# A new order of the transfers and of the first work in a fused S4 and gMLP block

## Chip, cores and metric

The kernel runs on one core of one Trainium2 chip. The metric is the time of one execution on the device, in microseconds (us); of several runs the median counts.

## What is computed

The reference, cut to the parts that matter here (`_A_ref` is a diagonal state-space layer as a convolution of length 2048, `_B_ref` a gated MLP with a 2048x2048 spatial mix):

```python
def _A_ref(u, A_re, A_im, B_re, B_im, C_re, C_im, log_dt, Dskip):
    dt = jnp.exp(log_dt)[:, None]
    P = jnp.exp((dt * A)[:, :, None] * l[None, None, :])
    K = jnp.einsum("dn,dnl,dn->dl", Cc, P, dB).real
    y = irfft(rfft(u) * rfft(K))[:L]
    return y + u * Dskip
mod = (_silu(c) @ w_mod).reshape(c.shape[0], 6, 1, -1)
sa, ca, ga, sb, cb, gb = mod
h = _layernorm(x) * (1 + ca) + sa
x = x + ga * _A_ref(h, ...)
h = _layernorm(x) * (1 + cb) + sb
x = x + gb * _B_ref(h, ...)
```

There are 2048 rows of 576 channels with 128 complex poles each; `w_mod` is 576 x 3456.

## The kernel before

The convolution is done as a transform in two stages of 32 and 64 points. The poles' parameters come in five groups of channels (four of 128, one of 64); `poles` turns them on VectorE and ScalarE into phases and logarithms of magnitudes, splits each into three bf16 parts and writes these to DRAM (`pa_d`, `pb_d`), from where `poles_load` fetches the tables `lb`, `lc`, `la` of one group. Group 0 is worked off by itself first, groups 1 to 3 together (432 columns wide) by the steps `q`.

Everything up to the tick loop (line 862) is the opening. Its work is listed by hand in the string `OPENING`, one short step after another, and each engine runs its instructions in exactly that order (line 154 pins it). The steps that matter:

- `mm k`, `me k`, `mo k`, `mf k`: modulation vector k: matmuls with `w_mod`, copy, matmul with ones, final form (`gar`, `cga`, `sga`). `ga`, `gb` split the shift into `gsp` (ScalarE) and a residual `sga` (VectorE), three and two times in turn.
- `w i b`: statistics of norm tile i (512 rows); on VectorE, or with i in `LN_ACT` on ScalarE. `r b`: rows of block b, scaled (VectorE). `h j t k`, `H`, `u`: first transform stage of two blocks on TensorE, its eviction to `st1o` on ScalarE, its write to DRAM from GpSimd's queue.
- `eA`, `eB` and `EA`, `EB`: exponents of 16 channels on TensorE, exponentials on ScalarE. `a`, `c` and `A`, `C`: phases on TensorE, sines on ScalarE. `pa`, `pb`: products on VectorE. `k`, `K`, `d`, `n`, `N`: the convolution's kernel and its transform.
- `q`: the next piece of the later poles, 22 in all. `X`: tables of group 1 (memsets and loads by GpSimd). `L`, `ml`: loads of norm tiles and of `w_mod`. `U`, `um`, `ue`, `us`, `zm`, `zv`, `vm`, `ve`: the first units of the second stage.

The units `mm`, `mo`, `eA`, `a`, `c` and `h` each take a PSUM tile `ps` of two banks (line 206), of which there are two; a unit's tile is free again when its eviction has read it. `eB`, `k`, `n` use four tiles `pk` of one bank. `st1o` has two buffers, one for each pair of `h`.

Two queues issue the loads: SP (SyncE) runs ahead of everything but what it waits for, and GpSimd (POOL) issues in program order between its memsets and writes.

Of the kernel before, what the change touches and what calls it, by code (L numbers as in the profile page):

```python
# [20 lines left out]
L = 2048  # L21
# [100 lines left out]
def body(tc, I, out):  # L122
    nc = tc.nc
    V, A, G, T, S = nc.vector, nc.scalar, nc.gpsimd, nc.tensor, nc.sync
    with ExitStack() as ctx:
        dram = ctx.enter_context(tc.tile_pool(name="dram", bufs=1, space=DRAM))
        keep = ctx.enter_context(tc.tile_pool(name="keep", bufs=1))

        x1_d = dram.tile([16, 128, D], F32, name="x1_d")

        consts_s = keep.tile([128, 4], F32, name="consts_s")
        V.memset(consts_s[:, 0:1], MAGIC)
        V.memset(consts_s[:, 1:2], math.pi / 2)
        V.memset(consts_s[:, 2:3], 1.0)
        V.memset(consts_s[:, 3:4], 0.0)
        mod_d = dram.tile([3, D], F32, name="mod_d")
        acc = keep.tile([128, 96], F32, name="acc")
        m = Mlp(tc, ctx, I, x1_d, dram, mod_d, acc, out)
        ssm(tc, I, x1_d, consts_s, dram, mod_d, m)
        m.phase_a()  # L140
        m.phase_b()
# [17 lines left out]
class Pinned:  # L159
# [4 lines left out]
            Pin(tc, e) for e in (tc.nc.vector, tc.nc.scalar, tc.nc.gpsimd, tc.nc.tensor, tc.nc.sync)]  # L164


LN_ACT = (2, )

OPENING = (
# [17 lines left out]


def ssm(tc, I, x1_d, consts_s, dram, mod_d, mlp):
    nc = tc.nc  # L190
    V, A, G, T, S = nc.vector, nc.scalar, nc.gpsimd, nc.tensor, nc.sync
# [3 lines left out]
    with ExitStack() as ctx:  # L195
# [17 lines left out]
        small = cp.tile([128, 6, 128], F32, name="small")  # L213
# [121 lines left out]
        def poles_load(c, Q, names=("lb", "lc", "la")):  # L335
            for n in names:
                d_, k = {"lb": (pb_d, 0), "lc": (pa_d, 0), "la": (pa_d, 3)}[n]
                for h in range(2):
                    Q.dma_start(lt[n, c][64 * h:64 * h + 48].rearrange("p g n -> p (g n)"),
                                d_[c, k:k + 6, h].rearrange("q (c g n) -> q c (g n)", c=8, g=9))  # L340
# [28 lines left out]
        def mod_load(k, Q):  # L369

            if k < 2:
                t = kp.tile([128, 32, 128], F32, name="k1").rearrange("p a b -> p (a b)")
                wmt[k] = [t[:96, 6 * HC * hh:6 * HC * hh + 6 * HC].rearrange("p (k n) -> p k n", k=6) for hh in range(2)]
            else:
                wmt[k] = [ep.tile([96, 6, HC], F32, name="wm") for hh in range(2)]
            for hh in range(2):
                Q.dma_start(wmt[k][hh], I["w_mod"][:, k, hh])
# [5 lines left out]
        msk = cp.tile([128, 2], F32, name="msk")  # L383
# [3 lines left out]
        def mod_mm(k):  # L387
            wm = wmt.pop(k)
            pm = md[k] = ps2()
            for hh in range(2):  # L390
                for kt in range(6):
                    j = kt % 4
                    T.matmul(pm[32 * j:32 * j + 32, hh, :HC], ec[:, kt:kt + 1].to_broadcast([96, 32]),
                             wm[hh][:, kt], start=kt < 4, stop=kt >= 2, skip_group_check=True)
# [36 lines left out]
        r1t = ep.tile([128, 16, 2, 32], F32, name="r1t", bufs=1)  # L431
        cst_ = ep.tile([128, 16, 2, 32], BF, name="cs", bufs=1)

        def ln_load(i, Q):
            x4s[i] = ep.tile([128, 4, D], F32, name="ln_x")
            Q.dma_start(x4s[i], I["x"][:, 4 * i:4 * i + 4])
# [5 lines left out]
        def ln_stat(i, b):  # L442
            x = x4s[i]
            if i in LN_ACT:
                if b == 0:
# [366 lines left out]
        V, A, G, T, S = mlp.tied.vector, mlp.tied.scalar, mlp.tied.gpsimd, mlp.tied.tensor, mlp.tied.sync  # L812
        p0 = poles(0, 1, G, tb.tile([128, 1536], F32, name="et", bufs=5))
        S.dma_start(cT, I["c"])
        mod_load(2, S)
        S.dma_start(sel[:112], I["c_sel"][:112])
        mod_load(1, S)
        S.dma_start(small, I["c_small"][:, 128:].rearrange("p (i c) -> p i c", i=6))
        S.dma_start(sel[112:], I["c_sel"][112:])
        poles_tile(0, G)  # L820
        for _ in range(4):
# [2 lines left out]
        for _ in range(12):  # L824
            next(p0)
        poles_load(0, S, ("lb",))
        ln_load(0, G)
        mod_mm(2)
        mod_ev(2)
        for _ in p0:  # L830
            pass
        poles_load(0, S, ("lc", "la"))
        p1 = poles(1, 4, G)
        mod_load(0, G)
        G.dma_start(r1t, I["c_r1t"])
        G.dma_start(cst_, I["c_cs"])
        G.dma_start(msk, I["c_msk"])
        ln_load(1, G)
        S.dma_start(dsk, I["dsk"])
        sb = cs = wpre = None  # L840
        steps = {"eA": e_mm, "EA": e_ex, "eB": ec_mm, "EB": ec_ex, "a": lambda g: phase(g, 1), "A": lambda g: sine(g, 1),
# [19 lines left out]
        V, A, G, T, S = nc.vector, nc.scalar, nc.gpsimd, nc.tensor, nc.sync  # L861
# [40 lines left out]
        V, A, G, T, S = mlp.nc.vector, mlp.nc.scalar, mlp.nc.gpsimd, mlp.nc.tensor, mlp.nc.sync  # L902
# [1427 lines left out]
```

## Time and profile before

| | before |
|---|---|
| median of 3 runs | 1771.0 us (1770.16 to 1778.1) |
| profiled execution | 1774.06 us, span 1772.2 us |
| PE busy | 1679.9 us (95%) |
| DVE busy | 1244.5 us (70%) |
| ACT busy | 820.3 us (46%) |
| POOL busy | 252.6 us (14%) |
| HBM read, written | 263.12 MB, 101.31 MB |

Busy is the time in which an engine had an instruction at work. The shares are averages over a kernel with several stages; what the opening is bound by has to be read from the opening alone, by windows of time and by the timeline. The chain of waits that ended last, which the page sums up, can be followed back only to 329.84 us and says nothing of the opening.

### The profile page before, as it was taken

The numbers are of one execution on the slowest core, as the hardware profiler recorded it, in microseconds if no ns is written. First come the engines' busy times: TensorE is split into PE (matmuls) and PEld (weight loads), VectorE is DVE, ScalarE is ACT, GpSimd is POOL, SyncE is SP. The second block draws the span as 40 slices with busy tenths as digits, with TensorE's granted clock in tenths as the row PEclk, the third lists the DMA queues.
The fourth block names the chain that finished last, engine by engine and source line by source line (L and its number), as shares of the span: only waits on it lengthen the run. The fifth ranks groups of instructions, "written<-read, shape, count | busy, mean of one in ns | idle before, by whom it ended". The sixth has DMA issues, their size and how long they took to land.

```text
span 1772.2 us, 36706 instructions
## 1 busy us (share of the span) xinstructions
PE 1679.9 (95%) x15374; PEld 1248.7 (70%) x15374; DVE 1244.5 (70%) x2242; ACT 820.3 (46%) x1095; POOL 252.6 (14%) x397
## 2 busy tenths in 40 slices
PE   4688999997899999999999999999999999999999
PEld 1355555565455545788878888888888888888887
DVE  5885698856999997788898767788334477344432
ACT  3587798844577666355533443333232223122210
POOL 2141442333122211000000000000111100111100
PEclk9999999998999999999999999999999999999999
DMA  8465846689588779777665886773766573556531
GB/s 244 140 174 170 245 119 173 187 219 315 186 267 270 242 239 292 256 269 248 225 204 172 311 290 234 252 247 123 250 228 224 192 232 98 195 203 216 188 111 41
DMA packets 181484, 376.28 MB, mean 212 GB/s; under 512 B 38341, under 2 KB 101445, under 8 KB 180550
## 3 DMA queue, kind: packets, MB, share of 16 engines
q1 hardware_dynamic: 137782, 171.43, 32.1%
q0 software_dynamic: 37632, 175.83, 29.9%
q10 hardware_dynamic: 5904, 26.67, 3.7%
q8 instruction: 121, 1.98, 0.5%
q14 instruction: 45, 0.37, 0.1%
HBM read 263.12 MB, written 101.31 MB: 206 GB/s over the span
## 4 chain that ended last, share of the span: by engine, by line
PE 55%; DVE 12%; issue 7%; DMA 5%; ACT 2%; POOL 1%; SPq 0%; ACTq 0%; DVEq 0%; POOLq 0%
PE ps L154 49%; PE pz L154 4%; DMA zset<-set_d 3%; DVE bsz L154 1%; DVE zset L154 1%; DVE wsp L154 1%; DVE n L154 1%; DVE gt L154 1%; DVE rq L154 1%; DMA uu<-v_d 1%; ACT z L154 1%; DVE nt L154 1%; DVE wso L154 1%; PE pk L722 0%; DVE rx L154 0%
## 5 line engine op out<-in xcount | busy, mean ns | idle before, releaser
L154 PEld LDWEIGHTS <-zset 128*128 128x128 f16 x7182 | 701.7, 98 | 94.5 <-DVE zset L154 7.4
L154 PE MATMUL ps<-wsp,zset 128*128 128x256 f16 x6048 | 667.6, 273 | 8.8 <-DVE zset L154 5.5
L154 PE MATMUL pz<-wz,nt 128*128 128x512 f16 (+1 forms) x1120 | 223.4, 360 | 8.6 <-DVE nt L154 4.2
L154 PEld LDWEIGHTS <-nt 128*128 128x128 f16 x1120 | 109.9, 99 | 115.8 <-DVE nt L154 5.7
L154 ACT ACTIVATE z<-gt 128x1024 f16<-128x1024 f32 x56 | 59.0, 1054 | 285.8 <-DVE gt L154 285.8
L2038 POOL DMA_DIRECT2D zset<-set_d x96 | 50.8, 530 | 871.2 <-PE ps L154 638.2
L154 DVE SCALAR_TENSOR_TENSOR gt<-ps,sc,bsp 128x512 f32<-128x512 f32 x36 | 27.0, 749 | 206.1 <-PE ps L154 204.4
L154 PE MATMUL ps<-wout,z 128*128 128x288 f16 x1344 | 170.0, 286 | 0.0
L154 PEld LDWEIGHTS <-z 128*128 128x128 f16 x1344 | 131.5, 98 | 33.0
L154 PE MATMUL ps<-n2o,zset 128*128 128x256 f16 x1134 | 128.3, 273 | 0.0
L154 DVE TENSOR_TENSOR raw<-raw 128x512 f32<-128x512 f32 (+2 forms) x228 | 119.0, 528 | 12.4 <-DMA raw<-z_d 8.1
L154 DVE SCALAR_TENSOR_TENSOR gt<-ps,sc,gt 128x512 f32<-128x512 f32 (+1 forms) x180 | 122.2, 696 | 7.6
L154 ACT ACTIVATE zset<-raw 128x1792 f16<-128x1792 f32 x48 | 81.2, 1691 | 60.5 <-PE ps L154 29.1
L154 DVE TENSOR_TENSOR zset<-raw,zset 128x1792 f16<-128x1792 f32 x48 | 96.9, 2019 | 15.4 <-ACT zset L154 15.4
L154 DVE TENSOR_TENSOR z<-ps,z 128x512 f32<-128x512 f32 (+1 forms) x126 | 71.9, 598 | 37.1 <-ACT z L154 26.7
L154 ACT ACTIVATE wsp<-raw,sc 128x1792 f16<-128x1792 f32 x25 | 44.6, 1785 | 43.1 <-DVE raw L154 35.2
L154 ACT ACTIVATE z<-pz,sc 128x512 f32<-128x512 f32 (+1 forms) x96 | 52.4, 579 | 19.3 <-PE pz L154 13.4
L154 ACT ACTIVATE z<-z,sc 128x1024 f32<-128x1024 f32 x21 | 24.1, 1149 | 75.9 <-DVE z L154 72.2
L154 PE MATMUL ps<-n2q,wf 128*128 128x512 f16 x252 | 55.7, 379 | 0.0
L154 ACT ACTIVATE z<-z,nm,r 128x1152 f32<-128x1152 f32 x24 | 31.5, 1342 | 51.4 <-DVE nm L154 28.9
L154 PE MATMUL ps<-wout,z1b 128*128 128x288 f16 x384 | 52.6, 286 | 0.5 <-ACT z1b L154 0.5
L154 DVE SCALAR_TENSOR_TENSOR wsp<-raw,sc,wsp 128x1792 f16<-128x1792 f32 x25 | 51.9, 2078 | 0.0
(353 smaller groups left out, 2447.9 us busy)
## 6 DMA issues: line engine op xcount, KB each, us to landing
zset<-set_d POOLq DMA_DIRECT2D x96, 896.0 KB, 4.9
raw<-z_d SPq DMA_DIRECT2D x48, 512.0 KB, 5.2
set_d<-zset ACTq DMA_DIRECT2D x24, 896.0 KB, 6.6
z_d<-z POOLq DMA_DIRECT2D x32, 576.0 KB, 9.0
zset<-wa_d POOLq DMA_DIRECT2D x18, 896.0 KB, 4.9
raw<-in_w_spT SPq DMA_DIRECT2D x25, 512.0 KB, 5.7
set_d<-zset SPq DMA_DIRECT2D x12, 896.0 KB
u_d<-st1o POOLq DMA_DIRECT2D x16, 576.0 KB, 4.2
```

The costliest lines, as they stand in the source:

```text
L154: return self.tc.keep_in_program_order(f(*a, **k))
L2038: self.nc.gpsimd.dma_start(o, self.set_d[f, j - 1] if j else self.wa_d[f])
```

## The change

The inputs that GpSimd's queue loaded (`x` of norm tiles 0 and 1, `w_mod` for modulation 0, and the constants `r1t`, `cs`, `msk`) are now issued from SP's, all in one order: behind `lb` the first norm tile, behind `la` the modulation and the constants, then the inputs of the later poles, and behind them the second norm tile. `r1t`, the norm's table of cosines, comes in two parts. `small` is ahead of modulation 1's matrix. Statistics of norm tile 0 instead of tile 2 run on ScalarE. `OPENING` has the same 396 steps (but for the statistics) in another order, of which the diff shows the line around the first norm units.

```diff
-LN_ACT = (2, )
+LN_ACT = (0, )
...
-    "q 0;r 0;a 0;me 0;q 1;mo 0;mf 0;q 2;c 0;ga 0;gb 0;q 3;ga 1;gb 1;q 4;r 1;w 1 0;r 2;ga 2;A 0;w 1 1;r 3;w 1 2;h 0 0 0;C 0;w 1 3;"
...
+    "w 0 5;w 0 6;w 0 7;w 0 8;EA 2;w 0 9;mm 0;EB 2;q 0;r 0;me 0;r 1;mo 0;r 2;mf 0;r 3;a 0;ga 0;gb 0;A 0;q 1;ga 1;c 0;gb 1;C 0;w 1 0;"
+    "ga 2;a 1;w 1 1;A 1;w 1 2;h 0 0 0;w 1 3;H 0 0 0;w 1 4;h 0 0 1;H 0 0 1;h 0 1 0;u 0 0;H 0 1 0;q 2;h 0 1 1;H 0 1 1;h 1 0 0;u 0 1;r 4;"
...
@@ -814,8 +814,8 @@
         mod_load(2, S)
         S.dma_start(sel[:112], I["c_sel"][:112])
+        S.dma_start(small, I["c_small"][:, 128:].rearrange("p (i c) -> p i c", i=6))
         mod_load(1, S)
-        S.dma_start(small, I["c_small"][:, 128:].rearrange("p (i c) -> p i c", i=6))
...
         poles_load(0, S, ("lb",))
-        ln_load(0, G)
+        ln_load(0, S)
...
         poles_load(0, S, ("lc", "la"))
+        mod_load(0, S)
+        S.dma_start(cst_, I["c_cs"])
+        S.dma_start(msk, I["c_msk"])
+        S.dma_start(r1t[:, :4], I["c_r1t"][:, :4])
         p1 = poles(1, 4, G)
-        mod_load(0, G)
-        G.dma_start(r1t, I["c_r1t"])
-        G.dma_start(cst_, I["c_cs"])
-        G.dma_start(msk, I["c_msk"])
-        ln_load(1, G)
+        ln_load(1, S)
+        S.dma_start(r1t[:, 4:], I["c_r1t"][:, 4:])
         S.dma_start(dsk, I["dsk"])
```

What this moves on the engines is seen in the order of their instructions. On SP's queue, behind the first inputs (`lb`, `lc`, `la` are the tables of pole group 0, `t_n_...` the inputs of the later poles, `k_239` the matrix of modulation 0), there stood before:

```order
L154 DMA lb<-pb_d 48x1x1152 x2
L154 DMA lc<-pa_d 48x1x1152 x2
L154 DMA la<-pa_d 48x1x1152 x2
L154 DMA t_n_log_dt<-in_A_log_dt 128x3x144
L154 DMA t_n_A_im<-in_A_A_im 128x3x144
```

and now, at the same place:

```order
L154 DMA lb<-pb_d 48x1x1152 x2
L154 DMA ln_x<-in_x 128x2304
L154 DMA lc<-pa_d 48x1x1152 x2
L154 DMA la<-pa_d 48x1x1152 x2
L154 DMA k_239<-in_w_mod 96x1728 x2
L154 DMA cs<-in_c_cs 128x1024
L154 DMA msk<-in_c_msk 128x2
L154 DMA r1t<-in_c_r1t 128x256
L154 DMA t_n_log_dt<-in_A_log_dt 128x3x144
```

The norm's first tile and the modulation's matrix have come in from POOL's queue, ahead of the later poles' inputs.

On ACT, from the later poles' first exponential to the first norm evictions (`et` exponentials, `gsp` the shift, `ft` sines, `st1o` the norm units' evictions, `t_n_B_...` the later poles' logarithms), there stood before:

```order
L154 ACTIVATE t_dt<-t_n_log_dt 128x432
L154 ACTIVATE mpart<-ps 128x576
L154 ACTIVATE gsp<-sga 128x576 x2
L154 ACT_TABLE_LOAD
L154 ACTIVATE t_dt<-t_n_B_re 128x432
L154 ACTIVATE t_q_360<-t_n_B_im 128x432
L154 ACTIVATE t_q_360<-t_q_360,consts_s 128x432
L154 ACTIVATE gsp<-sga 128x576
L154 ACT_TABLE_LOAD
L154 ACTIVATE ft<-ps 128x1024 x2
L154 ACTIVATE st1o<-ps 128x576
```

and now:

```order
L154 ACTIVATE t_dt<-t_n_log_dt 128x432
L154 ACTIVATE mpart<-ps 128x576
L154 ACTIVATE gsp<-sga 128x576
L154 ACT_TABLE_LOAD
L154 ACTIVATE ft<-ps 128x1024
L154 ACTIVATE gsp<-sga 128x576
L154 ACTIVATE ft<-ps 128x1024
L154 ACTIVATE gsp<-sga 128x576
L154 ACTIVATE ft<-ps 128x1024
L154 ACTIVATE st1o<-ps 128x576 x7
L154 ACTIVATE ft<-ps 128x1024
L154 ACTIVATE st1o<-ps 128x576
```

The later poles' logarithms have left this place, and the norm's evictions follow each other with almost no sine between them. The next exponential (`EA 3`) comes only behind three more sines, although its matmuls (`eA 3`) stand ahead of `mm 0`: it holds one of the two `ps` tiles all that time.

On POOL's queue, around the tables of group 1 (`X`: the memsets and the loads of `lb`, `lc`, `la`; `u_d<-st1o` are the norm units' writes), there stood before:

```order
L154 DMA u_d<-st1o 128x4x288
L154 MEMSET lb 32x1152
L154 MEMSET lc 32x1152
L154 MEMSET lc 17x1152
L154 MEMSET la 32x1152
L154 MEMSET la 17x1152
L154 DMA lb<-pb_d 48x1x1152 x2
L154 DMA lc<-pa_d 48x1x1152 x2
L154 DMA la<-pa_d 48x1x1152 x2
L154 DMA mod_d<-gar 16x1x36
L154 DMA u_d<-st1o 128x4x288 x2
```

and now:

```order
L154 DMA u_d<-st1o 128x4x288 x2
L154 DMA mod_d<-gar 16x1x36
L154 DMA pa_d<-pt 128x3x144 x3
L154 MEMSET lb 32x1152
L154 MEMSET lc 32x1152
L154 MEMSET lc 17x1152
L154 MEMSET la 32x1152
L154 MEMSET la 17x1152
L154 DMA lb<-pb_d 48x1x1152 x2
L154 DMA lc<-pa_d 48x1x1152 x2
L154 DMA la<-pa_d 48x1x1152 x2
L154 DMA u_d<-st1o 128x4x288 x2
```

Of the sixteen writes of norm units eight stood behind this step, and now two.

31 rows, old and new, of the table OPENING are left out of this document.

## Prediction

> **What bounds the kernel now.** I began with the page, in whose 40 slices TensorE (PE) is short of full only at the start, and went on to the windows of 20 us.
>
> ```profile
> span 1772.2 us, 36706 instructions
> PE   4688999997899999999999999999999999999999
> ```
> ```profile
> 20.00:40.00 20.00, 13.39 (x53) 5.01 (x57) 8.81 (x34) 7.53 (x11) 4.02 (x7) 1.00 0.98 282
> 40.00:60.00 20.00, 8.89 (x44) 3.79 (x37) 15.07 (x26) 6.44 (x11) 0.00 (x0) 1.00 0.55 137
> 160.00:180.00 20.00, 17.92 (x299) 9.87 (x297) 11.14 (x15) 16.25 (x24) 2.29 (x3) 0.91 0.75 242
> ```
> The columns are stretch, length, busy PE, PE weight loads, VectorE (DVE), ScalarE (ACT) and GpSimd (POOL), granted clock, DMA share, GB/s. From 20 to 40 the DMA engines are the bound (0.98). From 40 to 60 they are half free and PE still works only 8.89 of 20 us. After that PE is "busy" nearly throughout, but not always at the same speed, as the third fence below shows.
>
> The hole between 50 and 62 us is read from the timeline (start, length, engine, line, operation, tiles; in brackets the idle time before and its releaser):
>
> ```profile
> 54.48 2.85 DVE L154 RECIPROCAL t_rnd<-t_n_B_re 128x432 f32<-128x432 f32 x1
> 57.89 0.81 DVE L154 SCALAR_TENSOR_TENSOR sga<-gsp,msk,sga 128x576 f32<-128x576 bf16 x1
> 59.16 0.67 ACT L154 ACTIVATE gsp<-sga 128x576 bf16<-128x576 f32 x1
> 61.14 1.94 ACT L154 ACTIVATE ft<-ps 128x1024 f32<-128x1024 f32 x2
> 62.21 0.47 PE L154 MATMUL ps<-gsp,cs 32*64 32x288 bf16 x4 [11.95 <-ACT ft L154]
> ```
> The first norm matmul (`h 0 0 0`) waits 11.95 us for a PSUM buffer. Both `ps` buffers hold phases, whose sines (`ft`) stand on ACT behind the poles' logarithms, and these behind the poles' reciprocal on DVE.
>
> ```profile
> 67.49 0.47 PE L154 MATMUL ps<-gsp,cs 32*64 32x288 bf16 x4
> 69.01 0.65 ACT L154 ACTIVATE st1o<-ps 128x576 f32<-128x576 f32 x1 [0.55 <-PE ps L154]
> 64.49 0.61 PE L154 MATMUL ps<-sel 48*128 48x512 bf16 x2
> 66.42 1.02 ACT L154 ACTIVATE ft<-ps 128x1024 f32<-128x1024 f32 x1 [1.07 <-PE ps L154]
> 112.36 0.39 PE L154 MATMUL ps<-sel 48*128 48x512 bf16 x2
> 113.44 1.02 ACT L154 ACTIVATE ft<-ps 128x1024 f32<-128x1024 f32 x1 [0.29 <-PE ps L154]
> 91.16 0.33 PE L154 MATMUL ps<-gsp,cs 32*64 32x288 bf16 x4
> 98.00:104.00 6.00, 6.00 (x50) 3.73 (x52) 2.73 (x6) 4.12 (x8) 1.28 (x2) 0.50 0.41 142
> ```
> A norm unit takes 1.52 us from PE's start to its eviction (67.49 to 69.01), a phase 1.93 (64.49 to 66.42); later a phase takes 1.08 (112.36 to 113.44). Up to 91.16 the norm's matmuls take 0.47, there 0.33, and at 98 to 104 the granted clock is 0.50. So PE runs at half speed until about 91 us, and again in short stretches. (The column says 1.00 before 91; the durations don't, and I go by them.)
>
> The opening ends where the loop of ticks begins:
>
> ```profile
> 187.48 1.11 ACT L578 ACTIVATE ft<-ps,consts_s 128x1024 f32<-128x1024 f32 x1 [0.75 <-ACT ft L154]
> ```
> Behind it nothing changes, so what the opening gains or loses reaches the end. All of the sum is made there, against the profiled execution (1774.06 us, span 1772.2), which is 3 us above the median of 1771.0.
>
> **Part 1: the transfers.** Nothing is removed; seven POOL issues go to SP. The norm's first rows move from POOL at 18.01 to a place behind `lb`, whose issue waits for the poles' write.
>
> ```profile
> 18.01 0.57 POOL L154 DMA_DIRECT2D ln_x<-in_x  x1
> 25.07 0.82 DVE L154 BATCH_NORM_STATS2 bs<-ln_x 128x6 f32<-128x288 f32 x2 [3.06 <-DMA ln_x<-in_x]
> 22.47 1.65 SPq L154 DMA_DIRECT2D lb<-pb_d  x2
> 25.91 1.69 SPq L154 DMA_DIRECT2D la<-pa_d  x2
> k<-in_w_mod POOLq DMA_DIRECT2D x2, 648.0 KB, 8.6
> 38.78 4.06 PE L154 MATMUL ps<-k,ec 96*32 96x288 f32 x24
> ```
> They go out at 22.47 + 1.65 = 24.1. They took 7.06 us before (18.01 to 25.07); the bounds are 4.2 (1.18 MB at the 282 GB/s of that window) and 8.6 (what 1.33 MB of `w_mod` took). I take 7.06, the same transfer: they land at 31.2. The last modulation matrix (`mod_load 0`) goes out behind `la`, at 25.91 + 1.69 = 27.6, and with its 8.6 us lands at 36.2. What issuing costs SP (1.65 for the two `lb`) lies beside these transfers.
>
> The tile's statistics now stand on ACT, between the exponentials:
>
> ```profile
> 89.39 0.68 ACT L154 ACTIVATE ln_x<-ln_x 128x576 f32<-128x576 f32 x1
> 98.84 0.78 ACT L154 ACTIVATE mpart<-ln_x,nm 128x576 f32<-128x576 f32 x1
> 99.74 0.78 ACT L154 ACTIVATE mpart<-ln_x,nm 128x576 f32<-128x576 f32 x1
> ```
> Four sums of 0.68 and four squares 0.90 apart (98.84 to 99.74) are 6.3 us (7.2 if all are 0.90 apart). With a wide exponential (as wide as the sine's 1.02) and a half as wide one (0.6, an estimate from it) the chain ends at 31.2 + 6.3 + 1.6 = 39.1, and frees the PSUM buffer that the last modulation's matmuls (`mm 0`) take. They start at 39.1, against 38.78: **no gain from the transfers themselves**.
>
> **Part 2: from `mm 0` to the first norm matmul.**
>
> ```profile
> 44.38 0.63 ACT L154 ACTIVATE mpart<-ps 128x576 f32<-128x576 f32 x1
> 45.07 2.29 PE L154 MATMUL ps<-mpart,small 128*128 128x288 f32 x4 [0.36 <-ACT mpart L154]
> 47.57 0.75 DVE L154 TENSOR_TENSOR sga<-ps,gar 128x576 f32<-128x576 f32 x1
> 44.62 0.61 DVE L154 TENSOR_TENSOR t_n_A_im<-t_dt,t_n_A_im 128x432 f32<-128x432 f32 x1 [6.48 <-DMA t_n_A_im<-in_A_A_im]
> 59.84 1.28 ACT L154 ACT_TABLE_LOAD   x1
> ```
> In the new order: `mm 0` 4.06, its copy 0.63, ones matmul 2.29, `sga` 0.75, one row step on DVE (0.81 and a short operation, 1.06), `sga`'s residual 0.81 (at 57.89), then the poles' first six DVE operations 2.95 (44.62 to 47.57) and the second residual 0.81. ACT's part (table load 1.28, sine, `gsp` 0.67) fits beside these. Behind the residual stand a sine 1.02, the last `gsp` 0.67 beside the third phase 1.93, and its sine 1.02. With some 0.1 us at each of a dozen handovers that is 17.4, so `h 0 0 0` starts at 39.1 + 17.4 = 56.5, **5.7 us earlier**, with one exponential unit (1.1) and one phase (1.93) done besides. The logarithms have left this path; they now stand behind `h 3 0 0`.
>
> **Part 3: one PSUM buffer instead of two.** The fourth exponential's `ps` buffer is taken before `mm 0` and read only after `k 0`. Until then each unit waits for the eviction of the one ahead of it. A norm unit costs 1.50 + 0.65 + 0.05 = 2.2 us, a phase 1.93 + 1.02 + 0.05 = 3.0. Eight norm units and three phases are 26.6, so the last sine ends at 83.1, and `k 0`, 1.87 long behind the last phase's matmuls, at 83.9. The old order was there here:
>
> ```profile
> 82.62 0.61 PE L154 MATMUL ps<-sel,lb 48*128 48x512 bf16 x2
> ```
> So at the same point of the work the new order is **1.3 us later**; all of part 2 is given back. Were the units at full speed (1.08 for a phase) this stretch would be some 8 us shorter; were every eviction late by 0.3, 3 longer.
>
> **Part 4: behind that point.** ACT has as much left: eight statistics fewer (6.3), but a table load of 1.28 and eight of the poles' operations more (0.55 each, an estimate from 0.68 at 576 columns against their 432). That is +0, between −1 and +1. By 98 us DVE has 21 of the poles' operations more left (0.61 at most, as at 44.62: 12.8), and less by tile 2's root (15 operations of about 0.2) and three row steps: some 6.7 us more, in stretches where it idles 9 of 20 us (the row 160 to 180). I charge 2 (bounds 0 and 6.7). Walking both orders on from 83 us at these durations, PE has four norm units more done by 98, and one `k` unit (1.87) less: −2.2 (0 to −3.7). Then two waits go:
>
> ```profile
> 127.44 0.84 POOL L154 DMA_DIRECT2D u_d<-st1o  x1
> 136.90 0.65 ACT L154 ACTIVATE st1o<-ps 128x576 f32<-128x576 f32 x1 [2.55 <-DMA u_d<-st1o]
> 137.60 0.39 PE L154 MATMUL ps<-sel 48*128 48x512 bf16 x2 [2.15 <-ACT st1o L154]
> 138.00:142.00 4.00, 4.00 (x34) 1.85 (x34) 3.46 (x4) 2.23 (x3) 0.35 (x1) 0.61 0.01 4
> 188.66 1.98 PE L154 MATMUL pk<-zz,small 128*128 128x512 f32 x4 [1.16 <-DVE zz L154]
> 192.49 1.13 PE L736 MATMUL pk<-zz,small 128*128 128x512 f32 x2 [0.95 <-DVE zz L154]
> ```
> POOL's step for the second pole tile (`X`, its memsets and loads, up to 127) delayed a norm tile's write, whose buffer then held up ACT and PE, 2.15 us, and cost clock (0.61 over 4 us, 1.6 us lost). Only the last two writes stand behind `X` now: −3.8 (down to 0 if other loads slow such a write). The swaps of `uu` are issued some 25 steps further ahead of `zz`: −2.1.
>
> **The sum**: +1.3 + 2.0 − 2.2 − 3.8 − 2.1 = −4.8, say −5.
>
> A rule speaks against this change. The Trainium skill ("TensorE: Matmul & The Clock Gate", section "A second HAM failure mode: psum-queue depth-cycling") says that a PE which idles briefly between groups because it cycles through PSUM drops and regains its clock. The trace bears it out in that it runs at half speed from 62 to 91 us with shorter gaps than part 3 brings. By the rule the stretch of part 3 stays at half speed, as reckoned; without it, it would be 8 us shorter.
>
> **The rivals.**
> - **More gain.** The norm's rows land in 4.2 us, `mm 0` starts 2.9 us earlier (the matrix is there at 36.2), the DVE work costs nothing, and the half-speed stretch at 98 to 104 does not come back: −3. That is −4.8 − 2.9 − 2.0 − 3 = −12.7: 1758. For it: the DMA is in one order of need. Against: DVE's row steps must fit too.
> - **Nothing left.** DVE, with 6.7 us more to do, holds up `k` and row steps at full price (+4.7 on what I charged), or a norm tile's write is late beside another load (+3.8): 1770 to 1771. The change then does not do what it says: the poles' work is put off, and its wait comes with it. For it: DVE is busy 15.07 of 20 us at 40 to 60 even with PE idle. Against: 8.9 of 20 idle at 160 to 180.
> - **Slower.** After part 3 ACT sets the pace and PE's gaps go on, so that PE stays at half speed up to some 120 us, where before it had the full clock from 91.16 to 97.9 and from 104.9. A phase costs 0.85 more each time; about 20 us of work at full speed become some 36: +16 − 5 = 1782. It decides from 17 us of such work on (+14). For it: a pause of 2.15 was enough for 0.61 at 138. Against it: from about 92 us on phases, `k` and `n` units stand between the norm units, with two buffers again, as before.
>
> **How the numbers follow.** Forecast 1771 − 5 = 1766, chance 0.47, own range 1761 to 1770; more gain 0.25; nothing left 0.18; slower 0.10. About 0.5% (8.9 us) is what a measurement of this kernel can tell from no change: 1762.1 and 1779.9. Faster gets the second case and 0.05 of the first, 0.30; slower 0.11; the same 0.59. The range, 1754 to 1777, leaves out the end of the second case and the slower one.
>
> **What would show it.** In the new profile: `mm 0` near 39, `h 0 0 0` near 56 with no wait above 3 us; norm units 2.2 us apart up to about 83; no 2 us wait for `u_d` in ACT's evictions; the first L578 near 182. Wrong would be: the first rows landing well before 30, a norm pitch near 1.6 (full clock), or half-length durations missing beyond 105 us.

## The result, and the profile after

| | before | after |
|---|---|---|
| median | 1771.06 us (1770.16 to 1778.1, 5 runs) | 1786.72 us (1784.86 to 1792.18, 5 runs) |
| profiled execution | 1774.06 us, span 1772.2 us | 1789.75 us, span 1788.0 us |
| first instruction of the tick loop (L578) | 187.48 us | 205.93 us |
| granted clock from the end of part 3 to the tick loop | 0.93 over 104.9 us | 0.80 over 120.0 us |

After takes 1.0078 of before's time, 95% interval 1.0058 to 1.0098: 14 us slower by the ratio, 15.7 by the medians, where 5 faster was forecast. The page of after has nearly the same strip for PE as before:

```profile
span 1788.0 us, 36704 instructions
PE   4689999998899999999999999999999999999999
```

The windows of after (stretch, length, busy PE, PE loads, DVE, ACT, POOL, granted clock, DMA share, GB/s), the first two those that the prediction began with:

```profile
20.00:40.00 20.00, 10.52 (x36) 3.04 (x30) 2.17 (x7) 11.81 (x24) 0.75 (x1) 1.00 0.77 202
40.00:60.00 20.00, 13.44 (x76) 6.22 (x77) 15.88 (x52) 9.14 (x13) 0.00 (x0) 1.00 0.74 219
86.00:206.00 120.00, 107.85 (x1510) 59.67 (x1511) 77.63 (x152) 86.70 (x126) 35.47 (x50) 0.80 0.65 195
```

From 20 to 40 us the DMA engines, which were full before, are a quarter free; from 40 to 60 PE works 13.44 us in place of 8.89. The old hole is gone. What matters is the third row: behind 86 us PE is as busy as ever, at a lower clock. The same view of before, from the same point of the work (82.62) to its tick loop:

```profile
82.60:187.50 104.90, 93.50 (x1498) 53.23 (x1497) 67.05 (x133) 86.43 (x131) 30.25 (x43) 0.93 0.63 189
```

120 x 0.80 is 96.0 us of full clock and 104.9 x 0.93 is 97.6. At full clock the two stretches would be nearly alike; most of the 15.1 us between them is clock. Before's 0.93 is a little high, as the column reads 1.00 until it first records a change (at 98 us in before, while the matmuls up to 91 take their half-speed times; after's record begins at 90.6, and there this is under 1 us). The experiments below give 12.6 for the clock's part instead of 16.7.

After's timeline at the points that the prediction named (start, length, engine, line, operation; in brackets the idle time before it and its releaser):

```profile
33.64 0.68 ACT L154 ACTIVATE ln_x<-ln_x 128x576 f32<-128x576 f32 x1 [3.13 <-DMA ln_x<-in_x]
41.47 4.05 PE L154 MATMUL ps<-k,ec 96*32 96x288 f32 x24 [9.63 <-DMA k<-in_w_mod]
58.51 0.47 PE L154 MATMUL ps<-gsp,cs 32*64 32x288 bf16 x4 [1.11 <-ACT ft L154]
60.71 0.47 PE L154 MATMUL ps<-gsp,cs 32*64 32x288 bf16 x4 [0.77 <-ACT st1o L154]
84.04 0.44 PE L154 MATMUL pk<-pg 128*32 128x64 f32 x8
85.90 0.47 PE L154 MATMUL ps<-gsp,cs 32*64 32x288 bf16 x4
205.93 1.11 ACT L578 ACTIVATE ft<-ps,consts_s 128x1024 f32<-128x1024 f32 x1 [0.44 <-PE ps L577]
```

`mm 0` stands at 41.47, `h 0 0 0` at 58.51, norm units are 2.2 apart, and `k 0` runs from 84.04 to 85.90. Up to there the forecast holds within 2.4 us.

Where the clock goes, in after's windows:

```profile
90.00:100.80 10.80, 10.80 (x131) 5.50 (x130) 7.65 (x17) 9.53 (x14) 1.50 (x2) 0.53 0.29 112
111.90:131.00 19.10, 13.99 (x106) 6.69 (x100) 10.06 (x35) 7.86 (x12) 6.67 (x9) 0.57 0.55 195
138.40:152.50 14.10, 13.94 (x152) 7.68 (x153) 11.89 (x20) 9.31 (x15) 5.35 (x9) 0.52 0.60 171
193.00:200.00 7.00, 6.20 (x37) 4.56 (x37) 0.56 (x1) 5.87 (x7) 0.00 (x0) 0.51 1.08 303
```

PE has no gap in the first stretch, 0.2 and 0.8 us of gaps in the third and fourth, and runs at half speed all the same. Length times the clock that is missing gives 5.1 + 8.2 + 6.8 + 3.4 = 23.5 us. In the second it first stands still (some 1.4 of the 8.2 fall on this pause, where half speed costs nothing). The timeline there, by ACT, PE, POOL's and SP's queues:

```profile
116.65 1.19 ACT L154 ACTIVATE st1o<-ps 128x576 f32<-128x576 f32 x2 [5.28 <-DMA u_d<-st1o]
117.36 0.61 PE L154 MATMUL ps<-sel 48*128 48x512 bf16 x2 [5.11 <-ACT st1o L154]
...
105.87 0.75 POOL L154 DMA_DIRECT2D u_d<-st1o  x1 [3.11 <-ACT st1o L154]
...
103.14 1.28 SPq L154 DMA_DIRECT2D wm<-in_w_mod  x2
104.92 0.35 SPq L154 DMA_DIRECT2D ln_x<-in_x  x1
```

The eviction of `h 4 1 0` waits for the `st1o` buffer that `u 3 1` writes out. That write was issued at 105.87; the loads `ml 4` and `L 3` had gone out 2.7 and 0.9 us before. Its landing, by the view of DMA issues (operation, count, KB each, us to landing):

```profile
u_d<-st1o POOLq DMA_DIRECT2D x1, 576.0 KB, 10.7
```

In before the same stall exists once, 2.15 us of PE at 137.60. The write that it waits for, issued at 127.44, landed nearly as late, beside a modulation matrix that SP had issued at 125.87:

```profile
u_d<-st1o POOLq DMA_DIRECT2D x1, 576.0 KB, 9.4
```

So there were three suspects: the transfers, the PSUM buffer that `eA 3` holds, and this pause with the clock behind it.

### The profile page after: what moved, and what is told of

It reads as the page before. It is cut to its first block, busy times and chain, and to the rows that moved or that the text cites. A ratio compares the mean times of both kernels' runs of the same rounds, so it can differ in the third digit from the quotient of the medians.

```text
span 1788.0 us, 36704 instructions
## 1 busy us (share of the span) xinstructions
PE 1693.7 (95%) x15374; PEld 1253.9 (70%) x15374; DVE 1245.9 (70%) x2242; ACT 820.9 (46%) x1095; POOL 249.0 (14%) x390
## 4 chain that ended last, share of the span: by engine, by line
PE 52%; DVE 14%; issue 8%; DMA 5%; ACT 1%; POOL 0%; SPq 0%; ACTq 0%; POOLq 0%; DVEq 0%
PE ps L154 49%; DMA zset<-set_d 4%; DVE bsz L154 2%; DVE n L154 1%; DVE zset L154 1%; DVE rq L154 1%; DVE wso L154 1%; DVE gt L154 1%; PE pk L154 1%; DMA wst<-in_w_in 1%; DVE wsp L154 1%; DVE nt L154 1%; DMA z_d<-z 1%; DVE rx L154 1%; PE pk L722 1%
```

## The experiments

All ratios are against before's runs on the same chip (median 1775.9 to 1776.5 us here, 1771.06 in the result), so ratios are compared, not microseconds; 0.001 is 1.8 us.

**The two halves of the change.** `order_alone` is after with these lines of before, `transfers_alone` the reverse (before's list and `LN_ACT`, after's lines):

```diff
-        ln_load(0, S)
+        ln_load(0, G)
-        mod_load(0, S)
...
-        S.dma_start(r1t[:, :4], I["c_r1t"][:, :4])
-        ln_load(1, S)
-        S.dma_start(r1t[:, 4:], I["c_r1t"][:, 4:])
+        mod_load(0, G)
+        G.dma_start(r1t, I["c_r1t"])
...
+        ln_load(1, G)
```

> After's listed order and its choice of ScalarE for the first tile's statistics, with before's transfers (the norm's rows, the last modulation matrix and the small constants back on POOL's queue; the first rows in one piece). Theory C (the order makes the loss: behind k 0 PE runs at half speed in some 44 of 120 us, against some 15 of 105 before, and half of the difference is the 15 us): the time stays far above before's 1771, between 1781 and 1788; h 0 0 0 comes some 2 to 4 us earlier than in after (58.5), and the tick loop begins at 202 or later. Rival T (the transfers on SP land late and the rest shifts with them): 1766 to 1772, the tick loop near 187.

> After's transfers with before's listed order and before's tile for ScalarE's statistics. Theory C: only the front is touched (rows landing at 33.6 and not 25, the last modulation matrix at 41.5 and not 38.8), which costs 0 to 5 us: 1771 to 1776, and the granted clock behind 84 us stays as in before. Rival T: 1782 to 1788, with the loss in the first 60 us of the span.

Measured: `order_alone` 1.0089 (1.0067 to 1.0110), `transfers_alone` 1.0005 (0.9984 to 1.0025). The order makes the whole loss. The windows of `order_alone`, then of `transfers_alone`, over the stretches compared above:

```profile
86.00:206.00 120.00, 108.63 (x1500) 59.53 (x1500) 77.04 (x148) 86.44 (x125) 35.70 (x50) 0.79 0.64 195
```
```profile
82.60:187.50 104.90, 94.77 (x1498) 53.91 (x1497) 66.91 (x132) 86.33 (x130) 30.46 (x43) 0.88 0.62 188
```

In both runs the record of the clock begins before the stretch (at 31 and 50 us). The old order loses 104.9 x 0.12 = 12.6 us to the clock, the new one 120 x 0.21 = 25.2: 12.6 more.

**The held PSUM buffer.** `two_buffers` moves two steps of after's list:

```diff
-...;eA 2;EB 0;eB 2;EA 1;w 0 0;eA 3;w 0 1;eB 3;w 0 2;...;C 2;r 7;k 0;EA 3;...
+...;eA 2;EB 0;eB 2;EA 1;w 0 0;w 0 1;w 0 2;...;C 2;r 7;eA 3;eB 3;k 0;EA 3;...
```

> After with the fourth e-unit's two matmul steps (eA 3, eB 3) put just ahead of k 0, so that its PSUM buffer isn't held through the norm tiles; nothing else. Theory C1 (the single buffer of the norm stretch, with PE idle a third of the time, is what puts PE at half speed and costs 0.7 us at each of 8 norm units and 1.0 at each of 3 phases, 8.6 in all): h 0 0 0 to k 0 shrinks from 27.4 us to 19 to 21, the half-speed stretch at 90.6 to 100.8 is gone or shorter, and the time falls by 8 to 13: 1774 to 1779. Rival C2 (the stretch is paced by other things as well, the row steps on DVE above all, or what is won is given back at the late write of st1o, 5.3 us, which waits for its transfer): less than 4 us, 1783 to 1788.

Measured: 1.0014 (0.9993 to 1.0035), 0.0064 or 11 us under after (by the two intervals, give or take 5). Its timeline on PE:

```profile
55.56 0.33 PE L154 MATMUL ps<-gsp,cs 32*64 32x288 bf16 x4 [1.91 <-ACT gsp L154]
56.47 0.33 PE L154 MATMUL ps<-gsp,cs 32*64 32x288 bf16 x4
57.14 0.47 PE L154 MATMUL ps<-gsp,cs 32*64 32x288 bf16 x4
58.36 0.47 PE L154 MATMUL ps<-gsp,cs 32*64 32x288 bf16 x4
...
74.38 0.44 PE L154 MATMUL pk<-pg 128*32 128x64 f32 x8 [2.46 <-DVE pg L154]
```

`k 0` begins at 74.38, 9.7 us sooner (and is over at 78.1, 7.8 us sooner, as PE now waits for VectorE within it): 3.0 ahead of `h 0 0 0`, where the phases needn't go one by one either, and 6.7 in the norm stretch (18.8 us for 25.5). The clock is no part of that gain: the matmuls go from 0.33 to 0.47 at 57 us and the granted clock stays at half up to 94.5, though up to 72 PE has one gap of 0.8 us where after has one at every unit. And the second loss is all there, PE's wait at the late write (4.7 us) and the half speed behind it:

```profile
104.00:126.00 22.00, 16.93 (x174) 8.31 (x173) 13.38 (x40) 9.49 (x14) 7.59 (x11) 0.61 0.56 200
```

**The late write, a first try.** `loads_later` puts the two loads further back in the list, with the tile's statistics:

```diff
-...;me 3;ml 4;n 1;r 10;H 3 1 1;L 3;q 7;...;h 4 1 0;u 4 0;A 4;...;u 4 1;h 5 0 0;w 3 0;C 4;...
+...;me 3;n 1;r 10;H 3 1 1;q 7;...;h 4 1 0;u 4 0;L 3;A 4;...;u 4 1;ml 4;h 5 0 0;C 4;...;h 5 1 1;w 3 0;w 3 1;...
```

> After with the load of the fourth norm tile (L 3) put behind u 4 0 and the fourth modulation matrix (ml 4) behind u 4 1, and the tile's statistics (w 3) behind h 5 1 1; nothing else. In after ACT waits 5.3 us at 111 to 116.6 for the write of st1o, which lands 10.8 us after its issue beside these loads, and PE 5.1; the granted clock is 0.50 from about 115 to 131. Theory C (the wait and the clock that it costs): both go, 5 + 8 = 13 us: 1772 to 1776. Rival W (the wait alone is gained, the clock falls anyhow): 1780 to 1783. Rival N (the write waits behind some other transfer, or the late statistics hold up DVE): 1785 to 1789.

Measured: 1.0080 (1.0060 to 1.0099), no change. The timeline of SP's queue says why:

```profile
103.81 0.35 SPq L154 DMA_DIRECT2D ln_x<-in_x  x1
104.25 0.85 SPq L154 DMA_DIRECT2D wm<-in_w_mod  x2
```

SP does nothing else here. A load leaves as soon as its buffer is free, wherever it stands in the list; the edit only swapped the two. It tested nothing but my reading of the list.

**The late write, again.** `two_gated` is `two_buffers` with the list of `loads_later` and both loads on POOL, where they do wait behind the writes:

```diff
+                 "ml": lambda k: mod_load(k, G if k == 4 else S),
+                 "L": lambda i: ln_load(i, G if i == 3 else S),
```

> Two_buffers (ratio 1.0014) with the loads of the fourth norm tile (L 3) and the fourth modulation matrix (ml 4) really made to start later: they go to POOL's queue, behind the writes u 4 0 and u 4 1, and the tile's statistics (w 3) behind h 5 1 1. In loads_later the same steps stood on SP's queue, where nothing holds them, and were issued at 103.8 and 104.3 as ever. Theory L (the write of u 3 1 lands 10.7 us after its issue because these two loads run beside it): ACT's wait of 4.9 for u_d goes, and with it the half-speed stretch of 108 to 125.5: ratio 0.993 to 0.997, 8 to 13 us under two_buffers. Rival W (the wait goes and the clock falls anyhow): 0.998 to 0.9995. Rival N (the write waits behind something else, or a later write takes its place): 1.000 to 1.003.

Measured: 1.0012 (0.9993 to 1.0031), as rival N has it. The DMA views of its windows at 101 to 104 (`u 3 1`), 114 to 118 (`u 4 1`) and 118 to 122 (`ml 4`):

```profile
u_d<-st1o POOLq DMA_DIRECT2D x1, 576.0 KB, 3.4
...
u_d<-st1o POOLq DMA_DIRECT2D x1, 576.0 KB, 8.4
...
wm<-in_w_mod POOLq DMA_DIRECT2D x2, 648.0 KB, 7.9
```

Without a load beside it `u 3 1` lands in 3.4 us and not 10.7, so the loads do make it late. But `u 4 1` now shares the time with them, and with six writes of the later poles on the same queue, and ACT waits 6.85 us for that one.

`mm3_later` shifts the load of the modulation matrix by way of its buffer, on `two_buffers`:

```diff
-...;u 3 0;mm 3;H 3 1 0;q 5;d 1;q 6;h 3 1 1;me 3;ml 4;n 1;...;h 4 0 1;q 9;pa 3;a 4;H 4 0 1;K 2;...
+...;u 3 0;H 3 1 0;q 5;d 1;q 6;h 3 1 1;n 1;...;h 4 0 1;mm 3;q 9;pa 3;a 4;H 4 0 1;me 3;ml 4;K 2;...
```

> Two_buffers (ratio 1.0014) with mm 3 behind h 4 0 1, and me 3 and ml 4 behind H 4 0 1, so that the buffer which ml 4's load waits for comes free some 9 us later and the load starts there; L 3 as before. Theory L (the write of u 3 1 is slow since both loads run beside it): with L 3 alone beside it it lands in 5 to 8 us and not 10.7, ACT's wait falls from 4.9 to 0 to 3, and with a pause of PE under 2 us the clock holds: ratio 0.996 to 0.999. Rival N (another write is slow beside the shifted load, as in two_gated, where u 3 1 landed in 3.4 us but u 4 1, beside ml 4, in 8.4): 1.000 to 1.003.

Measured: 1.0004 (0.9988 to 1.0021), between the two: `u 3 1`, with `L 3` alone beside it, lands in 8.1 us, and the next write, beside `ml 4`, in 9.4. ACT's waits fall to 3.1 us in two, PE's to 1.0, and the time stays. Its timeline at the pause, then its windows:

```profile
104.39 0.61 PE L154 MATMUL ps<-sel 48*128 48x512 bf16 x2 [1.00 <-ACT st1o L154]
```
```profile
94.00:104.00 10.00, 9.01 (x176) 4.83 (x175) 8.98 (x18) 7.77 (x15) 4.24 (x6) 1.00 0.97 289
104.00:121.50 17.50, 17.11 (x178) 8.93 (x179) 10.16 (x31) 9.71 (x14) 4.53 (x7) 0.51 0.66 221
```

A pause of 1.0 us in place of 4.7, and the clock falls behind it for 17.5 us as it did behind the long one. "With a pause under 2 us the clock holds" was wrong.

**The clock alone.** The next runs leave every wait where it is and give PE something to do meanwhile. They add a step `f n`, n matmuls whose result nobody reads:

```diff
+        def fill(n):
+            t = ps1()
+            for _ in range(n):
+                T.matmul(t, lt["lb", 0][:, 0], sel[:112, 1024:1536], start=True, stop=True)
```

`fill_wait` is `two_buffers` with `f 20` behind `h 4 1 1`, `after_fill` is after with the same step and nothing else.

> Two_buffers (ratio 1.0014) with 20 matmuls whose result nobody reads (112 rows, 512 columns, bf16, 0.22 us apart at full clock: 4.4 us) behind h 4 1 1, where PE waits 4.7 us at 104.6 to 109.3. The wait itself stays. Theory C (PE's pause costs mostly through the clock that follows it): the granted clock stays at 1.00 over what was the half-speed stretch of 108 to 125.5, and some 8 us go: ratio 0.996 to 0.998. Rival P (the clock falls there with or without the pause, from the kind of work, norm units above all): 1.001 to 1.003, and the stretch is still there.

> After (ratio 1.0078) with the 20 unread matmuls behind h 4 1 1 and nothing else, so that the single PSUM buffer stays as it is and only PE's pause at 111.9 to 117.4 is filled. Theory C: the half-speed stretch of 114.5 to 131 goes, as it went in fill_wait: 5 to 9 us less, ratio 1.0025 to 1.005. Rival S (with the single buffer the clock is down from other pauses anyhow): 1.006 to 1.009.

Measured: `fill_wait` 0.9965 (0.9952 to 0.9979), 0.0049 under `two_buffers`; `after_fill` 1.0027 (1.0012 to 1.0043), 0.0051 under after: both some 9 us (by the intervals, give or take 4 to 5), and as theory C has it. The timeline of `fill_wait`, then its windows:

```profile
104.95 4.49 PE L154 MATMUL pk<-sel,lb 112*128 112x512 bf16 x20
109.72 1.19 ACT L154 ACTIVATE st1o<-ps 128x576 f32<-128x576 f32 x2 [5.57 <-DMA u_d<-st1o]
110.42 0.39 PE L154 MATMUL ps<-sel 48*128 48x512 bf16 x2 [0.98 <-ACT st1o L154]
```
```profile
104.00:126.00 22.00, 18.90 (x242) 9.61 (x245) 16.66 (x46) 14.82 (x24) 9.46 (x13) 1.00 0.74 245
126.90:140.50 13.60, 13.48 (x144) 7.51 (x145) 11.46 (x21) 7.76 (x13) 4.87 (x8) 0.50 0.48 149
```

ACT's wait is still there (5.57 us, 4.85 in `two_buffers`), PE goes on at 110.42 as in `two_buffers` (110.11), and from 104 to 126 the clock is 1.00 and not 0.61: 22 x 0.39 = 8.6 us, about 1 of it in the pause itself. `after_fill` has 1.00 from 111.9 to 131 where after has 0.57 (8.2 us):

```profile
111.90:131.00 19.10, 16.67 (x219) 8.41 (x216) 13.91 (x40) 13.55 (x21) 7.41 (x11) 1.00 0.71 235
```

`fill_both` adds `f 6` behind `eB 7`, `fill_three` also `f 2` behind `eB 8` and `f 3` behind `h 6 0 0`.

> Fill_wait (ratio 0.9965) with 6 more unread matmuls (1.3 us at full clock) behind eB 7, where PE waits 1.28 us for the evictions of the e-units and the clock falls 2 us later, from 126.9 to 140.5. Theory C: that stretch goes too, 13.6/2 = 6 to 7 us less: 0.992 to 0.994. Rival P (the clock falls there from the norm units that follow, or the matmuls push the e-units back as much): 0.996 to 0.998.

> Fill_both (ratio 0.9945) with 2 unread matmuls behind eB 8 and 3 behind h 6 0 0, where PE still waited 0.20 and 0.49 us and the clock fell from 125.1 to 135.5. If small pauses do it: the stretch goes, 5 us less, 0.990 to 0.993. If the kind of work does (norm units with phases between them): the stretch stays, 0.994 to 0.996.

Measured: `fill_both` 0.9945 (0.9925 to 0.9965), `fill_three` 0.9958 (0.9943 to 0.9972). The timeline of `fill_both`, and its window:

```profile
122.72 0.42 PE L154 MATMUL ps<-gsp,cs 32*64 32x288 bf16 x3 [0.20 <-ACT et L154]
...
124.12 0.33 PE L154 MATMUL ps<-gsp,cs 32*64 32x288 bf16 x4 [0.49 <-ACT et L154]
```
```profile
125.00:135.50 10.50, 10.50 (x124) 6.14 (x122) 9.26 (x16) 6.48 (x11) 2.63 (x4) 0.51 0.55 169
```

In `fill_both` the stretch is still there, behind pauses of 0.20 and 0.49 us, so theory C did not come true there (its number lies between the two forecasts). In `fill_three`, with these filled as well, it is gone, but the first half-speed stretch lasts longer, to 106.5, than in `fill_both`, to 91:

```profile
51.50:106.50 55.00, 48.62 (x535) 23.10 (x536) 43.48 (x104) 31.91 (x47) 6.07 (x8) 0.50 0.51 166
106.50:180.00 73.50, 69.94 (x1158) 38.66 (x1155) 53.39 (x101) 60.18 (x87) 31.83 (x45) 1.00 0.71 208
```

So the time did not fall, and this pair doesn't settle whether the small pauses or where the clock happened to rise made the difference.

**The same in the old order.** `before_fill2` fills before's own pauses: `f 2` behind `k 2`, `f 4` behind `a 3`, `f 5` behind `h 2 1 0`, `f 8` behind `c 7`.

> Before with unread matmuls where PE waits: 2 behind k 2, 4 behind a 3, 5 behind h 2 1 0 (waits of 0.55, 0.92 and 1.25 us at 93 to 98, after which the clock is at half from 97.9 to 105) and 8 behind c 7 (a wait of 2.15 at 135 to 137.6, half speed from 138.9 to 142.5). Theory C: both stretches go, 3.5 + 1.8 = 5 us less: 0.996 to 0.998. Rival P (they cost what they take, and the clock falls all the same): 1.000 to 1.003.

Measured: 0.9967 (0.9948 to 0.9985), as theory C has it; the half-speed stretches at 98 to 105 and 139 to 142.5 are gone, and so is a third one, at 176.5 to 180 in before, although the pause ahead of it (1.24 us) was left as it was:

```profile
97.90:105.00 7.10, 6.81 (x94) 3.81 (x93) 5.49 (x12) 7.00 (x16) 1.10 (x2) 1.00 0.61 193
105.00:190.00 85.00, 76.31 (x1245) 43.27 (x1248) 54.74 (x106) 66.83 (x94) 24.80 (x36) 1.00 0.72 213
```

With its pauses filled the old order stands at 0.9967, the new one (with two buffers) at 0.9945 to 0.9970, the last two runs below included. The intervals overlap: that the new order is the better one, once the clock is out of it, isn't shown. The traces don't show it either: the tick loop begins at 182.4 us in `before_fill2`, at 186.2 in `fill_both` and at 187.0 in `fill_three`, and their spans are 1765.2, 1768.8 and 1765.5.

**What raises the clock.** PE runs at half speed through the first norm units even without gaps. `fill_norm` (on `two_buffers`) and `before_fill` put one wide matmul, `f 1`, behind each of the first 8 norm units, to see whether these narrow matmuls are the reason.

> Two_buffers (ratio 1.0014) with one such matmul (112 rows, 512 columns) behind each of the 8 norm units of tiles 0 and 1. In two_buffers PE is busy without a gap from 55.6 to 72 and yet at half speed from 56.8 to 94.5. Theory K (the norm units, matmuls of 32 rows by 64 columns, keep the clock low even where they leave no gap, and wide matmuls between them would raise it): the clock rises some 10 to 20 us earlier than 94.5, and in spite of 8 x 0.43 = 3.4 us of added work at half speed the time falls by 2 to 6 us: 0.998 to 1.000. Rival G (gaps alone count, and the clock comes back only some 10 to 20 us after the last one at 72 to 78): the added work is paid, +1 to +4: 1.002 to 1.0035.

> Before with the same 8 matmuls behind its first 8 norm units, the last of which stands near 91 us. PE is busy there without a gap from 63 to 82 and its matmuls take the half-speed 0.47 to some 90 us. Theory K: the clock rises within 10 us of the first of them, and the time falls by 3 to 8 us: 0.9955 to 0.9985. Rival G: +1 to +4 us, 1.0005 to 1.0025.

Measured: 0.9998 (0.9983 to 1.0013) and 1.0009 (0.9991 to 1.0027). The number of `fill_norm` is the one that theory K named, but not for its reason: the clock came back at 107, later than the 94.5 of `two_buffers`. In its trace PE comes later to the slow write, ACT's longest wait for it is 1.9 us, and no half speed follows up to 127 us; that this is the gain is not tested. In `before_fill` the clock came back at 85, for 91 in before, but over 20 us behind the first of the added matmuls, where theory K had 10. Theory K falls, and neither run says what does raise the clock.

**The transfers again, with the pauses filled.** `best_sp` is `mm3_later` with `f 6` behind `h 4 1 1` and `eB 7`, `f 2` behind `eB 8`, `f 3` behind `h 6 0 0` and `f 4` behind `eB 11`; `best_pool` is that with before's transfers.

> Mm3_later (ratio 1.0004; in it PE waits 1.0 us at 104.4 and the clock is at half from 104 to 121.5, again from 127.9 to 138.5 and 179 to 189.5) with unread matmuls in its pauses: 6 behind h 4 1 1, 6 behind eB 7, 2 behind eB 8, 3 behind h 6 0 0, 4 behind eB 11. Theory C: the first stretch goes (17/2 = 8 us), and the others in part: 0.989 to 0.994. Rival: the clock falls anyhow, 0.999 to 1.001. After's transfers.

> The order and the matmuls of best_sp with before's transfers (first rows, last modulation matrix and small constants on POOL). If the transfers on SP only cost (first rows landing at 33.6 and not 25, last matrix at 41.5 and not 38.8 or less): 1 to 3 us under best_sp. If they make no difference: within 1.5 us of best_sp. If they gain (POOL's issues held up the poles): 1 to 3 us above.

Measured: 0.9967 (0.9954 to 0.9980) and 0.9970 (0.9955 to 0.9986). The transfers make no difference that can be measured, as in the two other pairs (before and `transfers_alone`, after and `order_alone`). The 0.989 to 0.994 of theory C was missed. `fill_both` has the lowest ratio of all, 0.9945, and is faster than both kernels; from the other filled runs its interval doesn't set it apart.

## Why the prediction was wrong

**Part 1** was mis-sized by 2.4 us. On SP the first rows took 10.0 us from issue to landing (23.63 to 33.64) and not 7.06, behind and beside the tables `lb`, `lc`, `la`; the last modulation matrix took 13.3 (28.19 to 41.47) and not 8.6. ACT's chain and the matrix came to the same end: `mm 0` at 41.47 for 39.1. "No gain from the transfers themselves" held.

**Part 2** came out: 17.04 us from `mm 0` to `h 0 0 0` for 17.4. But its listed terms add up to 17.3 without the handovers and to 18.5 with a dozen of 0.1 us, so the closeness is in part luck.

**Part 3** was right in mechanism and size: 2.2 us a norm unit, `k 0` over at 85.90 for 83.9, with all of the difference from part 1. The held buffer is thus no error of the sum, but it is the largest piece of the loss that can be taken away: set against before it looked like +1.3, while `two_buffers` reaches `k 0` 9.7 us sooner and is 11 us faster. Without it the new order would have been ahead of the old one here (`k 0` over at 78.1 for 82.6), and would have had something to lose. The rule of the Trainium skill that I weighed there ("TensorE: Matmul & The Clock Gate", "A second HAM failure mode: psum-queue depth-cycling") agrees with half speed in that stretch, but as its cause the gaps aren't borne out: `two_buffers` has one of them up to 72 us and stays at half speed up to 94.5, and before, which I read as bearing the rule out, has no gap above 0.15 us from 62.2 to 82.

**Part 4** is the step that failed: "behind that point" stood at −2.2 − 3.8 − 2.1 + 2.0 = −6.1. Of this the −2.1 for the swaps lies behind the start of the tick loop (before's waits for `zz` are at 188.66 and 192.49, L578 at 187.48). Up to the tick loop the forecast was thus −4.0, and it came out at +15.1. For the same reason "what the opening gains or loses reaches the end" is not exact: the tick loop begins 18.4 us later and the span ends 15.8 later.

The waits that were to go are gone, those for `zz` and the one behind `X`. The charge for VectorE and the gain in norm units can't be read one by one; at full clock the whole stretch takes 96.0 us for before's 97.6 (94.8 for 92.3 in `order_alone` and `transfers_alone`), −1.6 to +2.5 for the −4.0. The rest, 12.6 to 16.7 of the 15.1, is clock. What failed is that I walked both orders on at durations of before, that is at before's clock, and put the clock that new pauses cost at nothing. Pauses of 5.1, 1.4 and 2.4 us are followed in after by some 14, 14 and 7 us of work at half speed, and 10 more come behind part 3; before has 14 on record and some 8 ahead of its first record. The last of these pauses stands in the middle of one group of 16 matmuls:

```profile
191.60 0.60 PE L154 MATMUL pk<-small,kab 128*64 128x128 f32 x6 [2.37 <-issue]
```

PE waits there for nothing that the profile shows, and no run was made on it. Pauses of this kind come back in most runs of the new order (2.66 us in `two_buffers`, 1.54 in `fill_wait`), and before has none like it.

Two of the **rivals** had pieces of it. "Nothing left" had a norm tile's write that is late beside another load, at +3.8; it is 5.1, and it was priced without the clock that it takes along, another 8 to 9 (`fill_wait`, `after_fill`). "Slower" had half speed behind part 3 as its mechanism and 1782 as its time, at a chance of 0.10. It tied it to a steady pace of ACT, and was talked down with the two buffers that are back from 92 us on. But one pause is enough, as `after_fill` shows by filling it, and as the row at 138 to 142 of before, which I quoted for that rival, could have told. By that row the pauses of the new order should have been priced above their length, if only as a chance: behind before's two waits for `zz` (1.16 and 0.95 us) no half speed follows.

The 15.7 us of the result, put together from the runs: the held buffer 11, the clock behind the late write 9, and that wait some 3 more than the one of before; less 4.5 by which the order without the held buffer is ahead at the end of `k 0`, and 2.1 for the swaps: 16. That it comes so near is in part luck, since the 11 and the 9 are known to some 5 us each, since the other half-speed stretches of both orders are left out, and since removing one pause shifts when PE meets the next.

**Left open**: what raises the clock again, and which pauses make it fall; what PE waits for at 191.60; how much a new order is worth with no pause at all; and a way to keep the late write off the path, since of the two tries that reached it one moved the wait to another write and one left a pause that cost as much clock.

## What to carry to other kernels

A pause of TensorE can cost more than its length: here some pauses had a tail at half speed (at worst 27.5 us behind 1.24, in `before_fill`) and others of the same length had none. So an order is compared at full clock first, and then each remaining pause is priced with a possible tail. Where a pause can't be taken away, matmuls that nobody reads, issued ahead of the waiting one, are a cheap cure (0.5% here from twenty of them, in two kernels). And a buffer that is filled early and read late makes a double-buffered pool single for all that stands between: in a list written by hand, look for the producer that stands far ahead of its consumer.

## What the runs showed of the hardware

- The clock fell behind pauses of 1.00 us (`mm3_later`) and 1.28 us (`fill_wait`, ahead of its second stretch), and in `fill_both` behind 0.20 and 0.49. Yet `best_sp` kept it through a pause of 2.09; its timeline and its windows:

```profile
101.00 0.33 PE L154 MATMUL ps<-gsp,cs 32*64 32x288 bf16 x4 [2.09 <-ACT st1o L154]
```
```profile
94.00:117.50 23.50, 18.14 (x295) 9.39 (x287) 15.96 (x45) 14.35 (x25) 8.24 (x11) 1.00 0.82 262
117.50:121.00 3.50, 3.50 (x18) 1.71 (x17) 2.73 (x5) 1.84 (x4) 1.29 (x2) 0.51 0.43 169
```

  So the length of a pause alone doesn't decide. The Trainium skill ("TensorE: Matmul & The Clock Gate", "HAM oscillation — how this bites in real kernels") puts the limit for gaps at about 3.4 us; here the clock fell behind shorter ones too.
- Once down, it stayed at half for between 3.5 us (`best_sp`) and 27.5 us (`before_fill`, behind a pause of 1.24) of work nearly without a gap. Behind a much longer pause, 6.68 us at 117.5 in `two_gated`, it was 4.3 us. The window of `before_fill`:

```profile
102.00:129.50 27.50, 27.50 (x265) 13.21 (x265) 17.77 (x38) 16.98 (x28) 7.50 (x9) 0.51 0.58 176
```

  The same page of the Trainium skill ("What's actually happening") has about 3.4 us of busy time for the rise, in a window that runs on by itself; that fits only the shortest.
- The first half-speed stretch of the opening ended anywhere between 85 us (`before_fill`) and 108 us (`two_gated`, with 3.5 us at full clock on the way), with no rule to it that these runs show. In after, `loads_later` and `after_fill` the list is the same up to there, and the clock rose at 87, 86 and 100 us. Half of the whole spread, some 11 us, is as much as any effect studied here. Each trace is one execution: that of `before_fill`, at 1780.7 us, is near the top of its ten (1770.7 to 1781.0), and another may have other stretches.
- A write of 576 KB landed in 3.4 us with no load beside it (`two_gated`), and in 8.1 us (`mm3_later`) to 10.7 (after) beside loads of 1.2 to 2.5 MB; the 8.4 of `two_gated` had six small writes beside it as well.
